# Attention and Mish feed-forward on one core: loads one pair further ahead, and the first pair's q and k turned earlier

## The chip, the cores and the metric

The kernel runs on one NeuronCore of a Trainium2 chip. The metric is the device time of one execution in microseconds. A core has TensorE (PE), VectorE (DVE), ScalarE (ACT), GpSimd (POOL) and SyncE (SP); SP computes nothing here and issues most of the DMA transfers.

## The reference

```python
# q, k, v: (8, 12, 448, 64) float32; w_in: (768, 2048); w_out: (2048, 768)
scores = scale * np.matmul(q, k.transpose(0, 1, 3, 2))
m = np.max(scores, axis=-1, keepdims=True)
e = np.exp(scores - m)
attn = e / (np.sum(e, axis=-1, keepdims=True) + np.exp(-m) + 1e-09)
attn_out = np.matmul(attn, v)
x = attn_out.transpose(0, 2, 1, 3).reshape(3584, 768)
h = x @ w_in
g = h * np.tanh(softplus(h))      # Mish
out = g @ w_out                   # (3584, 768) float32
```

## The kernel before

The 96 heads are worked in 48 pairs, three pairs to a unit, so that a batch item is two units: units 0 to 15 hold attention, units 16 to 19 only what remains of the feed-forward. Units are counted from 0, so the eighth unit is unit 7. A unit u starts with pair p0 = 3u, and nxt = p0 + 3 is the first pair of the next unit.

**A pair's way in.** `load_pair` (line 158) issues three loads on SP's queue, one each for q, k and v, into buffers of which there are four of each kind. `cast_pair` (lines 201 to 207, with `cast_v`, 188) casts them to bf16 on GpSimd into `qk_bf`, which has room for six pairs. Then q and k must be turned so that the head's 64 channels lie on the partitions. That is done in one of two ways:

- `transpose_pair` (line 224) does eight transposes on TensorE into two PSUM banks, and `evac_qk` copies them out: q on VectorE, scaled (line 263), k on ScalarE (line 271).
- `turn_by_dma` (line 237) does it with one DMA transpose on SP's queue, straight from `qk_bf` to `qk_all`. `TURN_BY_DMA` lists the pairs for which it is used: every unit's first pair from pair 21 on, and pair 46.

`rest_of` (lines 245, 246) then makes on GpSimd two small copies that the fourth score step needs.

**The joined units.** Units 6 to 15 follow an order written out by hand, the list `JOINED`. Its entries are emitted one after the other: "s" the score matmuls of a step (lines 304, 307, 312), "m" the row maxima (line 335), "e" the exponentials (line 347), "fill" two matmuls' worth of the output product w_out (line 543), "copy" its evacuation (line 522) and, where rows are complete, the stores (line 507), "av" and "avc" the product with v of the unit before (line 423) and its evacuation (line 432), "load" a `load_pair` and, for arguments 1 and 2, a `cast_pair` one pair behind, "turn" a `turn_by_dma` if the pair is in the list. Every engine, and SP's queue, works off its own part in the order of emission.

**The Mish stage.** Behind the list come eight steps f = 0 to 7 of the product with w_in and Mish (lines 442, 469, 481). Into them are woven: at f = 0 the denominators (line 363) and the normalisation of the first pair on VectorE (line 386), and the DMA transpose of the normalised pair into `eT` (line 390) on SP; at f = 1, 3 and 5 the transposes and evacuations of the next unit's first, second and third pair, as far as they are not turned by DMA, and at f = 1 a `cast_pair`; at f = 3 the second pair's normalisation and the `rest_of` of a pair turned by DMA; at f = 4 the third pair's normalisation, which GpSimd does (line 384). Each normalisation is followed by its transpose into `eT`. At f = 7 the first three score steps of the next unit are emitted.

In a unit of even number, the first two steps of Mish are emitted together at f = 0 (`mm1_mish_first`), and f = 1 has no matmul of its own. In the joined units the PSUM bank of step f is given by a list, and the transposes go to banks 4 (q) and 2 (k) at f = 1 and 5, and to 5 and 3 at f = 3:

```python
    JOINED_MISH_BANK = (7, 0, 4, 2, 6, 1, 7, 6)
```

`LEAD` is 4. In the joined units before, "load" with argument a loads pair p0 + a + 3 and casts pair p0 + a + 2 (for a of 1 and 2); the cast at f = 1 is that of pair p0 + 5. So a unit loads and casts exactly the three pairs of the unit that follows.

Of the kernel before, what the change touches and what calls it, by code (L numbers as in the profile page):

```python
# [15 lines left out]
UNIT_PAIRS = 3  # L16
# [3 lines left out]
def kernel(  # L20
# [27 lines left out]
    N_PAIRS = B * HP  # L48
# [63 lines left out]
    for t_ in en_bufs:  # L112
# [4 lines left out]
    GROUP_FROM = 2 * HP  # L117
    JOINED_FROM = 2 * UNITS_PER_B + 2
    ONE_COPY = range(1, HP + UNIT_PAIRS)
    TURN_BY_DMA = tuple(  # L120
        p
        for p in range(GROUP_FROM + 3 * UNIT_PAIRS, N_PAIRS)
        if p % UNIT_PAIRS == 0 or p == N_PAIRS - UNIT_PAIRS + 1
    )
    SCALED_IN_CAST = (*ONE_COPY, *TURN_BY_DMA)
# [23 lines left out]
    def load_pair(p, which="qkv"):  # L149
        if p >= N_PAIRS:  # L150
            return
        b, h0 = p // HP, (p % HP) * 2
        tiles = loaded.setdefault(p, [])
        for nm, src in (("q", q), ("k", k), ("v", v)):
            if nm not in which:
                continue
            t = ld_pool.tile([SP_, 2, NT * D], FP32, tag=f"{nm}_f", name=f"{nm}_f")
            nc.sync.dma_start(
                out=t, in_=src[b, h0 : h0 + 2].rearrange("h (p t) d -> p h (t d)", t=NT)
            )  # L160
            tiles.append(t)
# [25 lines left out]
    def cast_v(p):  # L187
        nc.gpsimd.tensor_copy(out=casted[p][2], in_=loaded.pop(p)[2])  # L188

    def cast_pair(p, with_v=True):  # L190
        if p >= N_PAIRS:
            return
        q_f, k_f = loaded[p][:2]
        q_bf, k_bf = (qk_bf[:, p % N_CAST, i] for i in range(2))
        v_bf = bf_pool.tile([SP_, 2, NT * D], BF16, tag="v_bf", name="v_bf")
        by_t = "p h (t d) -> p t h d"
        cast_q, cast_k = nc.gpsimd.tensor_copy, nc.gpsimd.tensor_copy
        if p == 0:
            cast_q, cast_k = nc.vector.tensor_copy, nc.scalar.copy
        if p not in SCALED_IN_CAST:  # L200
            cast_q(out=q_bf, in_=q_f.rearrange(by_t, t=NT))  # L201
        else:
            nc.gpsimd.tensor_scalar(  # L203
                out=q_bf, in0=q_f.rearrange(by_t, t=NT),
                scalar1=SCALE, scalar2=1.0, op0=ALU.mult, op1=ALU.mult,
            )
        cast_k(out=k_bf, in_=k_f.rearrange(by_t, t=NT))  # L207
        casted[p] = (q_bf, k_bf, v_bf)
        if with_v:
            cast_v(p)  # L210
# [23 lines left out]
    def turn_by_dma(p):  # L234

        qk = qk_all[:, p % UNIT_PAIRS]
        nc.sync.dma_start_transpose(
            out=qk.rearrange("c s (t q) -> c (s t) q", q=SP_),
            in_=qk_bf[:, p % N_CAST].rearrange("q s t h d -> q (s t h d)"),
        )  # L240
        qkT[p] = qk[:, 0, :], qk[:, 1, :]
# [40 lines left out]
    def scores(idx):  # L282
        score_maxima(*score_products(idx))
# [45 lines left out]
    def score_maxima(st, s, at, heads=(0, 1)):  # L329
        sc, cols = st["sc", s]  # L330
        maxima = [(st["negm"][:, c : c + 1], sc[bk][:, 0:S]) for bk, c in enumerate(cols) if bk in heads]
        if len(cols) == 2 and sc_pairs[at] is not None:
            maxima = [(st["negm"][:, s : s + 5 : 4], sc_pairs[at][:, :, 0:S])]
        for negm, scored in maxima:
            nc.vector.tensor_reduce(out=negm, in_=scored, axis=AX.X, op=ALU.max, negate=True)  # L335
# [22 lines left out]
    def expm_of(p):  # L358
        w = att[p]["whole"]
        nc.scalar.activation(out=w["expm"], in_=w["negm"], func=AF.Exp)  # L360
# [205 lines left out]
    first_mm2 = 2 * UNITS_PER_B  # L566
# [5 lines left out]
    for g in range(B // 2):  # L572
# [51 lines left out]
    )  # L624
    JOINED = (
        ("mA", 1), ("fill", 2), ("mA", 0), ("fill", 1), ("mB", 0), ("fill", 1), ("eA", 1),
        ("load", 0), ("mB", 1), ("fill", 2), ("eA", 0), ("mB", 2), ("fill", 1), ("eB", 1),
        ("mA", 2), ("fill", 2), ("eB", 0), ("fill", 1), ("copy", 0), ("fill", 3), ("eB", 2),
# [4 lines left out]
        ("fill", 1), ("mB", 6), ("fill", 1), ("eA", 4), ("fill", 1), ("copy", 1), ("s", 11),  # L633
        ("eB", 6), ("load", 2), ("fill", 1), ("m", 11), ("fill", 1), ("eB", 5), ("fill", 1),
# [4 lines left out]
    )  # L639
# [12 lines left out]
    LEAD = UNIT_PAIRS + 1  # L652
# [68 lines left out]
    for u in range(UNITS_PER_B, N_UNITS + 2 * UNITS_PER_B):  # L721
# [10 lines left out]
        nxt = p0 + UNIT_PAIRS  # L732
# [5 lines left out]
        for what, arg in JOINED if joined else ():  # L738
            at, idx = p0 + arg, p0 * STEPS + arg
            heads = {"A": (0,), "B": (1,)}.get(what[-1], (0, 1))  # L740
            if what == "s":
                held[arg] = score_products(idx)
            elif what[0] == "m":
                score_maxima(*held[arg], heads)
            elif what[0] == "e":
                exps(idx, heads)
            elif what == "fill":
                for _ in range(arg):
                    filler.popleft()[0]()
            elif what == "copy":  # L750
                for evac in copies[arg]:
                    evac()
            elif what == "av":
                held["av", arg] = av_pair(at - UNIT_PAIRS, bank=joined_banks[AV_BANK[arg]])
            elif what == "avc":
                held["av", arg]()
            elif what == "load":
                load_pair(at + LEAD - 1)
                if arg:
                    cast_pair(at + LEAD - 2)  # L760
            elif nxt + arg in TURN_BY_DMA:
                turn_by_dma(nxt + arg)
        if joined:
            expm_of(nxt - 1)

        for n in () if joined else range(steps):
            pi, s = divmod(n, STEPS)
            p, idx = p0 + pi, p0 * STEPS + n
# [4 lines left out]
            if grouped:  # L773
# [14 lines left out]
                if n in LOAD_AT:  # L788
                    at = p0 + LOAD_AT.index(n)
# [51 lines left out]
        for f in range(FF_U):  # L841
            first_scores = f == FF_U - 1 and to_group and nxt < N_PAIRS
            if first_scores and u + 1 < JOINED_FROM:
                for s in range(3):
                    scores(nxt * STEPS + s)
            if moe:
                first = to_group and nxt == GROUP_FROM
                bank, ff = sc_banks[0][0] if f == 1 else None, w * FF_U + f
                if joined:
                    bank = joined_banks[JOINED_MISH_BANK[f]]  # L850
                elif to_group:
                    at = (FIRST_MISH_BANK if first else MISH_BANK)[f]
                    if at is not None:
                        bank = (sc_banks[0][1], None, mo_tiles[1], sc_banks[0][0])[at]
                if not joined or w or f >= MISH_AHEAD:
                    mm1_mish(b, FIRST_ORDER[f] if first else ff, bank)
                elif f == 0:
                    mm1_mish_first(b, [joined_banks[at] for at in JOINED_MISH_BANK[:MISH_AHEAD]])
                if f == 2 and to_gather:
                    gather_mid(to_gather.popleft())  # L860
            if first_scores and u + 1 >= JOINED_FROM:
                held = {s: score_products(nxt * STEPS + s) for s in range(3)}
            if u == UNITS_PER_B and f == 2:
                load_w(5)
            if not attn:
                continue
            if f == 0:
                denominators(att[p0]["whole"])
                normalise(todo[0], dma=todo[0] not in BY_PE)
            if f in (1, 3, 5):  # L870
                if nxt + f // 2 not in TURN_BY_DMA:
                    transpose_pair(nxt + f // 2, bank=f // 2 % 2)
                    evac_qk(nxt + f // 2)
                if f == 1 and u >= first_mm2:
                    cast_pair(nxt + UNIT_PAIRS - 1)
            if not to_group and f in (4, 6):
                scores_ahead(nxt * STEPS + f // 2 - 1)
            if f == FF_U - 1 and not to_group:
                scores_ahead(nxt * STEPS + 3)
            if f == 3:  # L880
                normalise(todo[1], dma=todo[1] not in BY_PE)
                for p in TURN_BY_DMA:
                    if p // UNIT_PAIRS == u + 1:
                        rest_of(p)
            if f == 4:
                normalise(todo[2], dma=todo[2] not in BY_PE, on_pool=u + 1 < N_UNITS)
# [39 lines left out]
```

## Time and profile before

| | us |
|---|---|
| median of three runs | 461.14 (459.6 to 462.93) |
| the profiled execution | 464.11 |
| its span, first to last instruction | 462.3 |
| TensorE busy | 427.4 |
| ScalarE busy | 342.1 |
| VectorE busy | 340.9 |
| GpSimd busy | 187.3 |
| mean granted TensorE clock | 0.987 of full speed |

In the rows of the profile "PE b L442 x6" means six matmuls from line 442 that write a tile named b; the number ahead is the start in us from the span's start, the next the time that the group took. In brackets stands the idle time of the engine before it, and what ended that. In the table by stretches each row has the stretch, its length, then busy time and count of PE, PEld, DVE, ACT and POOL, the granted clock, the DMA engines' busy share and GB/s. The ends of matmuls are modelled and overlap the next one's start, so start-to-start distances say more than durations.

### The profile page before, as it was taken

How to read it: one execution, taken by the hardware profiler on the slowest of the kernel's cores; microseconds unless marked ns; L12 is line 12 of the kernel's file. 1: busy time of each engine (PE TensorE's matmuls, PEld its weight loads, DVE VectorE, ACT ScalarE, POOL GpSimd, SP SyncE). 2: the span in 40 equal slices, each digit the busy share in tenths (PEclk: the TensorE clock that was granted, in tenths of full speed). 3: DMA queues.
4: the chain of work that ended last, by engine and by line, in shares of the span. 5: the costliest groups of instructions: out<-in, count | busy, mean ns of one | idle time of the engine just before them, and what ended most of it. 6: DMA issues, size and time to landing. Idle time of an engine off the chain costs nothing.

```text
span 462.3 us, 8732 instructions
## 1 busy us (share of the span) xinstructions
PE 427.4 (92%) x2968; PEld 234.3 (51%) x2968; DVE 340.9 (74%) x756; ACT 342.1 (74%) x908; POOL 187.3 (41%) x352
## 2 busy tenths in 40 slices
PE   4596798869999999899999999999999999999996
PEld 2243445434545655455555555455555455555565
DVE  4899978948887888868788888788888888421121
ACT  5998978967797979778888788798988888311300
POOL 4666655652616253353627171625454360000000
PEclk9997999999999999999999999999999999999999
DMA  8999999999999999999999999999999995950213
GB/s 229 207 200 221 255 151 215 221 199 216 195 246 238 207 210 204 264 194 278 199 244 231 219 234 209 271 206 238 227 270 205 255 203 137 171 137 0 69 35 102
DMA packets 211661, 92.66 MB, mean 200 GB/s; under 512 B 168352, under 2 KB 208160, under 8 KB 211616
## 3 DMA queue, kind: packets, MB, share of 16 engines
q1 hardware_dynamic: 204032, 85.76, 87.9%
q0 software_dynamic: 7488, 6.29, 9.4%
q8 instruction: 23, 0.38, 0.4%
q14 instruction: 22, 0.18, 0.1%
q10 hardware_dynamic: 96, 0.05, 0.0%
HBM read 45.61 MB, written 11.01 MB: 122 GB/s over the span
## 4 chain that ended last, share of the span: by engine, by line
PE 65%; DMA 16%; DVE 5%; ACT 5%; issue 3%; SPq 3%; POOL 2%; POOLq 0%; DVEq 0%; ACTq 0%
PE mo L543 25%; PE mo L442 15%; DMA q_f<-in_q_dram 7%; PE b L442 6%; PE b L543 5%; PE b L304 4%; ACT en L347 4%; DMA k_f<-in_k_dram 4%; DMA eT<-en 4%; DVE negm L335 3%; PE b L423 2%; PE mo L423 2%; PE b L224 2%; DMA qk_all<-qk_bf 1%; SPq L390 1%
## 5 line engine op out<-in xcount | busy, mean ns | idle before, releaser
L347 ACT ACTIVATE en<-b,negm 128x448 bf16<-128x448 f32 x216 | 133.9, 636 | 25.7 <-DVE negm L335 25.7
L335 DVE TENSOR_REDUCE negm<-b 128x1 f32<-128x448 f32 x216 | 120.9, 616 | 20.0 <-PE b L307 20.0
L543 PE MATMUL mo<-w_out_sb,gT 128*128 128x384 bf16 (+3 forms) x736 | 108.7, 300 | 1.4 <-DVE o_sb L522 0.7
L543 PEld LDWEIGHTS <-gT 128*128 128x128 bf16 x896 | 82.6, 98 | 51.8 <-issue 10.8
L442 PEld LDWEIGHTS <-w_in_sb 128*128 128x128 bf16 x768 | 72.3, 98 | 66.5 <-issue 5.5
L442 PE MATMUL mo<-xT,w_in_sb 128*128 128x448 bf16 x480 | 101.1, 353 | 0.8 <-DVE xT L432 0.3
L481 ACT ACTIVATE gT<-mo 128x448 bf16<-128x448 f32 x73 | 40.3, 552 | 52.1 <-PE mo L442 52.0
L384 POOL TENSOR_SCALAR en<-en,rden 128x448 bf16<-128x448 bf16 x109 | 67.3, 634 | 19.5 <-DVE rden L378 11.8
L386 DVE TENSOR_SCALAR en<-en,rden 128x448 bf16<-128x448 bf16 x227 | 71.8, 386 | 0.7
L442 PE MATMUL b<-xT,w_in_sb 128*128 128x448 bf16 x282 | 58.7, 352 | 0.0
L347 ACT ACTIVATE en<-sc,negm 128x448 bf16<-128x448 f32 x84 | 52.5, 642 | 3.9 <-DVE negm L335 2.6
L522 DVE COPY o_sb<-mo 128x384 f32<-128x384 f32 (+3 forms) x54 | 25.8, 494 | 40.1 <-PE mo L543 39.4
L335 DVE TENSOR_REDUCE negm<-sc 128x2 f32<-128x896 f32 (+1 forms) x48 | 45.4, 969 | 6.4 <-PE sc L307 4.0
L203 POOL TENSOR_SCALAR qk_bf<-q_f 112x512 bf16<-112x512 f32 x18 | 11.1, 615 | 88.1 <-DMA q_f<-in_q_dram 88.1
L347 ACT ACTIVATION_READ_ACCUMULATOR en<-b,negm 128x1 f32 x216 | 45.0, 208 | 0.0
L201 POOL CAST qk_bf<-q_f 112x512 bf16<-112x512 f32 x29 | 19.7, 679 | 44.6 <-DMA q_f<-in_q_dram 44.2
L188 POOL CAST v_bf<-v_f 112x512 bf16<-112x512 f32 x48 | 30.1, 626 | 15.0 <-DMA v_f<-in_v_dram 14.7
L207 POOL CAST qk_bf<-k_f 112x512 bf16<-112x512 f32 x47 | 29.3, 623 | 7.6 <-DMA k_f<-in_k_dram 6.4
L423 PEld LDWEIGHTS <-v_bf 112*64 112x64 bf16 x384 | 20.1, 110 | 23.4 <-issue 9.0
L224 PEld LDWEIGHTS <-qk_bf 112*128 112x128 bf16 x304 | 19.6, 104 | 21.7 <-POOL qk_bf L207 4.6
L304 PE MATMUL b<-qk_all 64*128 64x448 bf16 x108 | 29.3, 358 | 0.3 <-DMA qk_all<-qk_bf 0.3
L307 PE MATMUL b<-qk_all 64*128 64x448 bf16 x108 | 29.3, 358 | 0.0
(71 smaller groups left out, 524.7 us busy)
## 6 DMA issues: line engine op xcount, KB each, us to landing
q_f<-in_q_dram SPq DMA_DIRECT2D x48, 224.0 KB, 5.4
k_f<-in_k_dram SPq DMA_DIRECT2D x48, 224.0 KB, 5.6
v_f<-in_v_dram SPq DMA_DIRECT2D x48, 224.0 KB, 5.6
w_in_sb<-in_moe_w_in_dram POOLq DMA_DIRECT2D x12, 256.0 KB, 6.3
w_out_sb<-in_moe_w_out_dram POOLq DMA_DIRECT2D x8, 384.0 KB, 6.9
out_dram<-o_sb SPq DMA_DIRECT2D x7, 336.0 KB, 5.2
out_dram<-o_sb SPq DMA_DIRECT2D x8, 288.0 KB, 4.9
out_dram<-o_sb SPq DMA_DIRECT2D x8, 240.0 KB, 5.2
```

What stands on the lines that cost most here:

```text
L188: nc.gpsimd.tensor_copy(out=casted[p][2], in_=loaded.pop(p)[2])
L207: cast_k(out=k_bf, in_=k_f.rearrange(by_t, t=NT))
L304: nc.tensor.matmul(sc[0][:, 0:S], lhsT=qT[0:64, qa : qa + 128], rhs=kA, start=True, stop=True)
L307: nc.tensor.matmul(sc[1][:, 0:S], lhsT=qT[64:128, qb : qb + 128], rhs=kB, start=True, stop=True)
L335: nc.vector.tensor_reduce(out=negm, in_=scored, axis=AX.X, op=ALU.max, negate=True)
L347: nc.scalar.activation(out=st["en"][:, :, c, 0:SP_], in_=sc[bk][:, 0:S].rearrange("q (j c) -> q j c", j=NT), func=AF.Exp, bias=st["negm"][ ...
L384: nc.gpsimd.tensor_scalar(scalar2=1.0, op0=ALU.mult, op1=ALU.mult, **args)
L386: nc.vector.tensor_scalar(scalar2=None, op0=ALU.mult, **args)
L423: nc.tensor.matmul(av[h * 64 : (h + 1) * 64, 0:S], lhsT=v_bf[:, h, j * D : (j + 1) * D], rhs=e_h, start=(j == 0), stop=(j == NT - 1),)
L442: nc.tensor.matmul(h_ps[:, 0:S], lhsT=w_in_sb[:, dm, ff * 128 : (ff + 1) * 128], rhs=xT[b][:, dm, :], start=(dm == 0), stop=(dm == DM_T - 1),)
L481: nc.scalar.activation(out=gT[b][:, ff, :], in_=h_ps[:, 0:S], func=AF.Mish)
L543: nc.tensor.matmul(st["o"][:, st["at"] : st["at"] + nq * NQ], lhsT=src[:, ff, c0 : c0 + 128], rhs=w_out_sb[:, ff, q0 * NQ : (q0 + nq) * NQ ...
```

## The change

Four things are edited, and they hang together.

1. Pair 21, the first pair of unit 7, leaves the list of pairs turned by DMA; unit 6 transposes it on TensorE at f = 1.
2. In `JOINED`, ("turn", 0) moves from near the end to just behind ("s", 3), and ("load", 0) moves from near the start to right behind it. On SP's queue the turn then follows the three transposes into eT, and the loads follow the turn.
3. From unit 7 on a "load" loads one pair further ahead, p0 + a + 4, and casts p0 + a + 3; the cast at f = 1 is that of pair p0 + 6. So the first pair of a unit is loaded and cast one unit earlier than the others.
4. Unit 6 makes up for the step: at ("turn", 1) it loads pair 24, and at f = 1 it casts pairs 23 and 24.

```diff
-        for p in range(GROUP_FROM + 3 * UNIT_PAIRS, N_PAIRS)
+        for p in range(GROUP_FROM + 4 * UNIT_PAIRS, N_PAIRS)
...
         ("mA", 1), ("fill", 2), ("mA", 0), ("fill", 1), ("mB", 0), ("fill", 1), ("eA", 1),
-        ("load", 0), ("mB", 1), ("fill", 2), ("eA", 0), ("mB", 2), ("fill", 1), ("eB", 1),
+        ("mB", 1), ("fill", 2), ("eA", 0), ("mB", 2), ("fill", 1), ("eB", 1),
         ("mA", 2), ("fill", 2), ("eB", 0), ("fill", 1), ("copy", 0), ("fill", 3), ("eB", 2),
-        ("fill", 3), ("s", 3), ("eA", 2), ("fill", 1), ("m", 3), ("s", 5), ("s", 4), ("s", 6),
+        ("fill", 3), ("s", 3), ("turn", 0), ("load", 0), ("eA", 2), ("fill", 1), ("m", 3), ("s", 5),
+        ("s", 4), ("s", 6),
...
-        ("eA", 10), ("av", 0), ("avc", 1), ("eA", 8), ("turn", 0), ("av", 2), ("avc", 0),
+        ("eA", 10), ("av", 0), ("avc", 1), ("eA", 8), ("av", 2), ("avc", 0),
...
             elif what == "load":
-                load_pair(at + LEAD - 1)
+                lead = LEAD - 1 if u == JOINED_FROM else LEAD
+                load_pair(at + lead)
                 if arg:
-                    cast_pair(at + LEAD - 2)
+                    cast_pair(at + lead - 1)
             elif nxt + arg in TURN_BY_DMA:
                 turn_by_dma(nxt + arg)
+            elif u == JOINED_FROM and arg == 1:
+                load_pair(nxt + UNIT_PAIRS)
...
-                if f == 1 and u >= first_mm2:
+                if f == 1 and first_mm2 <= u <= JOINED_FROM:
                     cast_pair(nxt + UNIT_PAIRS - 1)
+                if f == 1 and u >= JOINED_FROM:
+                    cast_pair(nxt + UNIT_PAIRS)
```

## The prediction

> **What bounds the kernel now.** I read the busy table first, then the stretches of the joined stage one unit at a time, then the waits of TensorE.
>
> ```profile
> PE 427.4 (92%) x2968; PEld 234.3 (51%) x2968; DVE 340.9 (74%) x756; ACT 342.1 (74%) x908; POOL 187.3 (41%) x352
> ```
>
> TensorE is the engine to watch. The share alone doesn't say where it waits, so I cut the span at the first score matmul (line 304) of each unit. Each row below is one unit, units 6 to 14; after the length stands TensorE's busy time.
>
> ```profile
> 149.00:173.41 24.41, 24.41 (x175) 13.55 (x175) 21.11 (x48) 20.91 (x56) 9.93 (x21) 1.00 1.00 208
> 173.41:199.84 26.43, 24.74 (x175) 13.47 (x175) 20.53 (x47) 21.01 (x56) 12.22 (x24) 1.00 1.08 235
> 199.84:224.63 24.79, 24.47 (x174) 13.54 (x174) 20.72 (x48) 21.19 (x57) 10.05 (x19) 1.00 1.08 214
> 224.63:249.81 25.18, 24.74 (x173) 13.38 (x174) 21.07 (x47) 20.73 (x56) 12.06 (x25) 1.00 1.13 245
> 249.81:274.36 24.55, 24.55 (x174) 13.56 (x174) 20.96 (x48) 21.02 (x56) 11.74 (x23) 1.00 1.03 228
> 274.36:299.52 25.16, 24.57 (x174) 13.55 (x174) 21.01 (x47) 21.02 (x56) 11.65 (x24) 1.00 1.16 236
> 299.52:324.32 24.80, 24.58 (x175) 13.49 (x175) 21.16 (x48) 21.01 (x56) 9.95 (x20) 1.00 1.08 219
> 324.32:348.71 24.39, 24.39 (x174) 13.59 (x173) 20.55 (x47) 20.91 (x56) 12.31 (x26) 1.00 1.11 251
> 348.71:373.48 24.77, 24.35 (x166) 13.08 (x166) 21.18 (x47) 20.57 (x55) 11.44 (x22) 1.00 1.11 233
> ```
>
> Units 6 and 13 last 24.41 and 24.39 us and TensorE is busy through all of them: 24.39 us is the floor of a unit with two pairs transposed on TensorE. The others are longer by 2.04, 0.40, 0.79, 0.16, 0.77, 0.41 and, in unit 14, 0.38. That is the whole pool from which earlier loads can pay. What it consists of is seen where the long unit 7 stops, and at the start of unit 9:
>
> ```profile
> 193.91 1.30 PE L442 MATMUL b<-xT,w_in_sb 128*128 128x448 bf16 x6
> 196.71 0.37 PE L224 MATMUL b<-ident,qk_bf 112*128 112x112 bf16 x4 [1.50 <-POOL qk_bf L201]
> ...
> 190.87 0.61 POOL L201 CAST qk_bf<-q_f 112x512 bf16<-112x512 f32 x1
> 195.58 1.07 POOL L201 CAST qk_bf<-q_f 112x512 bf16<-112x512 f32 x1 [2.79 <-DMA q_f<-in_q_dram]
> ...
> 224.63 0.36 PE L304 MATMUL b<-qk_all 64*128 64x448 bf16 x1 [0.32 <-DMA qk_all<-qk_bf]
> ```
>
> The transposes of a unit's third pair wait for GpSimd's cast, the cast for its load; once the scores wait for the turned pair. The chain of waits agrees: in this stage it runs through loads, casts and the turn wherever it leaves TensorE.
>
> **What the change takes away.** From unit 7 on, the third pair to be transposed gets its cast at the place of the second one before: in unit 7 that is 190.87 instead of 195.58, against a need at 195.04 (six matmuls from 193.91, 0.19 us each, which is 1.13). Even 1.3 us later it would be in time. The turn is issued some 8 us earlier. So all seven excesses should go: 2.04 + 0.40 + 0.79 + 0.16 + 0.77 + 0.41 + 0.38 = 4.95. Unit 14 has one pair fewer on TensorE and its own floor lies lower by the step of eight transposes, 0.39 (the first two rows of the next fence): together **5.3 us gained**. The lower end is 3 us, if only the waits that TensorE's rows name go.
>
> **What it adds in unit 6.** Pair 21 leaves the list of pairs turned by DMA. Its eight transposes now stand in the Mish stage of unit 6 behind f = 1, write banks 4 and 2 of the joined banks, and are evacuated by VectorE (q, line 263) and ScalarE (k, line 271). The next matmuls in program order, f = 2, write bank 4 again, and f = 3 bank 2 (JOINED_MISH_BANK). In no unit of the trace from 6 on did transposes stand there, so the cost is worked out from the order of the engines:
>
> ```profile
> 167.98 0.56 PE L224 MATMUL b<-ident,qk_bf 112*128 112x112 bf16 x8
> 168.37 1.30 PE L442 MATMUL mo<-xT,w_in_sb 128*128 128x448 bf16 x6
> ...
> 165.14 3.00 PE L442 MATMUL b<-xT,w_in_sb 128*128 128x448 bf16 x15
> ...
> 165.51 0.63 ACT L347 ACTIVATE en<-b,negm 128x448 bf16<-128x448 f32 x1
> 166.73 0.23 ACT L360 ACTIVATE expm<-negm 128x21 f32<-128x21 f32 x1
> ...
> 166.99 0.18 DVE L363 SCALAR_TENSOR_TENSOR den<-sums,expm 128x21 f32<-128x21 f32 x1 [1.15 <-ACT expm L360]
> 167.53 2.90 DVE L386 TENSOR_SCALAR en<-en,rden 128x448 bf16<-128x448 bf16 x7
> ...
> 167.97 0.62 POOL L201 CAST qk_bf<-q_f 112x512 bf16<-112x512 f32 x1 [1.00 <-DMA q_f<-in_q_dram]
> ...
> 268.43 1.89 DVE L386 TENSOR_SCALAR en<-en,rden 128x448 bf16<-128x448 bf16 x7
> 270.58 0.38 DVE L263 TENSOR_SCALAR qk_all<-b 128x448 bf16<-128x448 bf16 x1
> ```
>
> Of the fifteen matmuls from 165.14 the first three belong to f = 0; f = 2 starts at 165.14 + 3 x 0.19 = 165.71. There the new transposes go in: q at once, k after the second-last exp (ends near 166.1) has read bank 2. VectorE reaches the evacuation only after the denominators (166.99, behind expm) and the seven normalisations of the first pair (line 386), which are emitted at f = 0. Those take 2.90 us here beside GpSimd's casts, 1.89 us in unit 10, where GpSimd was idle for most of them. After the change GpSimd has rest_of(21), which needs that same evacuation, queued ahead of the cast at 167.97, so it sits idle: I take 1.89. Evacuation 169.4 to 169.75, f = 2 at about 169.8: **4.1 us lost**, 0.39 of it work. Upper end 5.1 with 2.90; no lower end, since VectorE works in order. Behind it the extra cast of pair 24 on GpSimd and its three loads (in the place of the turn of pair 21 on SP) lie beside TensorE's later f's; k's evacuation at 169.2 on ScalarE precedes f = 3. No idle time follows in unit 6 that could absorb it.
>
> **The clock.** A gap that long costs more than itself in one place of this trace:
>
> ```profile
> 97.90:101.60 3.70, 0.04 (x1) 0.00 (x0) 1.06 (x3) 3.32 (x12) 1.47 (x3) 1.00 1.24 221
> 102.50:105.90 3.40, 3.40 (x14) 1.15 (x13) 1.40 (x3) 0.11 (x1) 0.00 (x0) 0.50 1.11 206
> ...
> 194.69:198.10 3.41, 1.72 (x15) 0.85 (x14) 2.38 (x8) 1.51 (x4) 2.46 (x5) 1.00 1.23 214
> ```
>
> After 3.7 us without matmuls the granted clock was 0.50 for 3.4 us (1.7 us of work lost); after unit 7's gap of 1.67 us it stayed 1.00. Ours is 4.1 us with eight transposes at its head. Ends 0 and 1.7; I take **1.0 lost**, since part of the slow stretch can fall inside the gap. The Trainium skill, page "TensorE: Matmul & The Clock Gate", section "Part 1: The HAM clock gate", says that the array falls to half rate after an idle window of about 3.4 us, and that the window runs free of the kernel; the 3.7 us row agrees. By that rule the fall hangs on where the window lies in each execution, so that the sum below would be 0.7 us higher with a full fall and 1.0 lower with none.
>
> **What it moves.** In SP's queue the turn now stands between the last eT transpose and the loads; load 0 stands behind it. SP and DMA are close to full there:
>
> ```profile
> 279.04 4.90 SPq L390 DMA_TRANSPOSE eT<-en  x1
> 284.00 0.57 SPq L158 DMA_DIRECT2D q_f<-in_q_dram  x1
> ...
> 259.43 0.58 SPq L158 DMA_DIRECT2D q_f<-in_q_dram  x1
> 267.37 1.34 SPq L237 DMA_TRANSPOSE qk_all<-qk_bf  x1
> ...
> 270.08 1.05 POOL L201 CAST qk_bf<-q_f 112x512 bf16<-112x512 f32 x1 [1.36 <-DMA q_f<-in_q_dram]
> ...
> 295.19 0.61 POOL L201 CAST qk_bf<-q_f 112x512 bf16<-112x512 f32 x1 [2.26 <-DMA q_f<-in_q_dram]
> 298.67 4.31 POOL L384 TENSOR_SCALAR en<-en,rden 128x448 bf16<-128x448 bf16 x7
> ...
> 286.87 1.68 PE L423 MATMUL mo<-eT,v_bf 112*64 112x448 bf16 x16
> ...
> eT<-en SPq DMA_TRANSPOSE x43, 6.8
> ```
>
> This is a ring: last eT transpose ends (283.94), nine loads, the third one cast (295.19: 11.2 us; in unit 10, 259.43 to 270.08, 10.7), then GpSimd normalises (3.5 later), 4.3, and the next last eT transpose can be issued, 4.9. That is 23.4 to 23.9 us. The turn now stands in it with 1.3: 24.7 to 25.2 us, against TensorE's 24.39. So the last eT comes later by 0.3 to 0.85 us in each unit, six times from unit 8 on: 1.8 to 5.1 us. The slack that it eats first: issued 279.04, landed 6.8 later at 285.8, wanted by the last eight of the sixteen matmuls from 286.87, at 287.6: 1.8 us. Left: 0 to 3.3; I take **1.0 lost**, nearer the lower end, since GpSimd also stops waiting for the turn itself. No wait of SP is new: the turn's target in qk_all is free after ("s", 3), some 5 us into a unit, while SP gets there 9 us in; its cast is one unit old. The f = 1 cast holds up the same things on GpSimd as before.
>
> **Sum.** +4.1 + 1.0 + 1.0 - 5.3 = **+0.8 us**. On the profiled execution, 464.11 us with a span of 462.3, that is 464.9; the median of the three runs is 461.14, 3 us lower, so I forecast **461.9 us**. One per cent, 4.6 us, is about what can be told from no change.
>
> **Rivals.**
> 1. *The ring becomes the bound.* If a turn between the transposes and the loads holds the DMA up by more than its 1.3 us of issue, say 2.3, the ring takes 25.7 to 26.2 and the period with it. It decides from 24.39 us on, once the 1.8 us are eaten: 6 x (1.3 to 1.8) - 1.8 = 6 to 9 lost in place of 1.0, +5.8 to +8.8 in all: 467 to 470. For it: DMA shares of 1.03 to 1.16 in every unit. Against it: the eT is nowhere waited for in units 7 to 14. Chance 0.15.
> 2. *The stall in unit 6 is not there or is covered*, for instance if VectorE gets to the evacuation sooner than I read. Then -5.3 + 1.0, at best -5.3: 455.8 to 456.8. Against it: VectorE's order. Chance 0.08.
> 3. *The change doesn't do what it says*: the casts stay late, as each waits in GpSimd's queue for loads that start 1.3 us later behind the turn, and only 1 to 2 us of the 5.3 go. Then +4 to +5: 465 to 466. Against it: the second cast's margin in unit 7, whose q is done at 191.48, with k's behind it, 3 us ahead of the need. Chance 0.07.
>
> The forecast with its own terms (clock 0 to 1.7, ring 0 to 3.3, stall to 5.1) has 0.70, and 459.9 to 465.9. To hold 8 in 10 I let the range run from 458.8 to 466.0. Faster by over 1% (under 456.5) 0.05, slower by over 1% (over 465.75) 0.17, within 0.78.
>
> **What would show it.** In unit 6 of the changed trace: a gap of TensorE of 3 to 4 us before f = 2, its releaser VectorE's line 263, and a clock row of 0.5 behind it or none. Units 7 to 14 at 24.4 us, no waits of line 224 for qk_bf. The last eT of a unit creeping towards the matmuls of line 423; waits of line 423 for eT would show the ring. The forecast is wrong if unit 6 shows no gap, or if units 8 to 14 stay above 24.8.

## The result and the profile after

The changed kernel takes 466.6 us (median of 20 runs), the kernel before 463.12 us in the runs beside it. The ratio is 1.0076 with a 95% interval of 1.0054 to 1.0099: 0.8% slower, some 3.5 us.

The whole loss can be read from the stage that was edited. This is the table by stretches of the changed kernel, units 6 to 14, cut as before at each unit's first score matmul:

```profile
147.67:177.74 30.07, 26.80 (x182) 14.52 (x182) 20.42 (x49) 21.78 (x57) 13.95 (x28) 0.94 0.99 210
177.74:202.14 24.40, 24.40 (x174) 13.54 (x174) 20.74 (x47) 20.91 (x56) 9.35 (x20) 1.00 0.88 203
202.14:226.54 24.40, 24.40 (x174) 13.58 (x174) 21.26 (x45) 21.02 (x56) 9.26 (x18) 1.00 1.16 230
226.54:251.90 25.36, 24.66 (x175) 13.62 (x175) 22.46 (x50) 21.04 (x56) 11.55 (x23) 1.00 1.11 232
251.90:276.87 24.97, 24.77 (x175) 13.61 (x175) 21.99 (x49) 20.93 (x56) 10.54 (x22) 1.00 1.04 220
276.87:301.73 24.86, 24.57 (x175) 13.57 (x175) 21.17 (x50) 20.91 (x56) 10.95 (x22) 1.00 1.11 235
301.73:326.48 24.75, 24.75 (x174) 13.63 (x175) 21.58 (x44) 21.03 (x56) 11.88 (x23) 1.00 1.07 235
326.48:351.96 25.48, 24.57 (x174) 13.53 (x173) 22.57 (x52) 21.02 (x56) 11.32 (x24) 1.00 1.10 230
351.96:376.04 24.08, 24.08 (x166) 13.31 (x167) 21.24 (x49) 20.54 (x55) 11.18 (x24) 1.00 1.07 211
```

Unit 6 went from 24.41 to 30.07 us: 5.66 lost. Units 7 to 14 went from 200.07 us together (173.41 to 373.48) to 198.30 (177.74 to 376.04): 1.77 won. That is +3.89 us. A unit with two pairs on TensorE takes 24.39 us where nothing is waited for, and unit 14 takes 24.00; by that the floor of units 7 to 14 is 194.73 us, and they stand 3.57 us over it. Outside the stage the two executions differ by -1.33 ahead of unit 6 and +0.24 behind unit 14, which leaves the 2.8 us between the spans, 462.3 and 465.1.

What TensorE waits for from 140 us on, in the waits of the changed kernel (line of the waiting work, releaser, us in total, times, longest; idle times under 0.15 us are left out):

```profile
PE b L442 <- DVE qk_all L263: 3.1, 1, 3.1
PE b L304 <- DVE qk_all L263: 1.9, 3, 0.9
PE b L423 <- DMA eT<-en: 0.9, 1, 0.9
```

The waits of transposes for casts are gone from the list. Both new waits are for VectorE's evacuation of q, line 263. The third one lies behind unit 14 and was there before. The list counts too little, because the modelled end of one matmul hides the start of a wait. Start to start, against units 7 and 8, the scores slip by 0.87, 0.28, 0.45 and 1.07 us in units 9, 10, 11 and 13, 2.67 us in all; the products with v slip by 0.5 us behind eT, and one transpose by 0.19 us behind its cast (unit 12). These are nearly all of the 3.57 us.

The first new wait stands in unit 6. TensorE, then VectorE, in order of time, then the stretch behind the gap:

```profile
164.38 0.36 PE L224 MATMUL b<-ident,qk_bf 112*128 112x112 bf16 x4
164.95 0.36 PE L224 MATMUL b<-ident,qk_bf 112*128 112x112 bf16 x4 [0.21 <-ACT en L347]
168.36 4.11 PE L442 MATMUL b<-xT,w_in_sb 128*128 128x448 bf16 x12 [3.05 <-DVE qk_all L263]
172.31 0.56 PE L224 MATMUL b<-ident,qk_bf 112*128 112x112 bf16 x8
...
166.20 1.81 DVE L386 TENSOR_SCALAR en<-en,rden 128x448 bf16<-128x448 bf16 x7
167.93 0.38 DVE L263 TENSOR_SCALAR qk_all<-b 128x448 bf16<-128x448 bf16 x1
...
168.30:171.80 3.50, 3.44 (x11) 1.44 (x11) 0.34 (x2) 0.58 (x2) 3.30 (x7) 0.55 1.06 157
```

The transposes begin at 164.38, where f = 2 would have begun, and f = 2 begins at 168.36: 3.98 us. Its twelve matmuls (f = 2 and 3) then reach to 172.31, which is 3.95 us instead of 2.27, at a granted clock of 0.55: another 1.68 us. Together they are the 5.66.

The second new wait is met first in the scores that are emitted at the end of unit 8 (in the table, the start of unit 9). TensorE, VectorE and GpSimd of the changed kernel, and at the end the normalisation's step over units 7 to 14, before and changed (behind the first bar the busy time in us and the mean of one in ns):

```profile
226.54 0.36 PE L304 MATMUL b<-qk_all 64*128 64x448 bf16 x1
227.80 0.35 PE L304 MATMUL b<-qk_all 64*128 64x448 bf16 x1 [0.70 <-DVE qk_all L263]
...
221.09 2.87 DVE L386 TENSOR_SCALAR en<-en,rden 128x448 bf16<-128x448 bf16 x7
224.51 2.86 DVE L386 TENSOR_SCALAR en<-en,rden 128x448 bf16<-128x448 bf16 x7
227.37 0.38 DVE L263 TENSOR_SCALAR qk_all<-b 128x448 bf16<-128x448 bf16 x1
...
221.48 0.66 POOL L201 CAST qk_bf<-q_f 112x512 bf16<-112x512 f32 x1 [0.78 <-DMA q_f<-in_q_dram]
224.92 0.64 POOL L203 TENSOR_SCALAR qk_bf<-q_f 112x512 bf16<-112x512 f32 x1 [1.33 <-DMA q_f<-in_q_dram]
...
L386 DVE TENSOR_SCALAR en<-en,rden 128x448 bf16<-128x448 bf16 x112 | 36.7, 396 | 0.3
L386 DVE TENSOR_SCALAR en<-en,rden 128x448 bf16<-128x448 bf16 x112 | 41.7, 441 | 0.3
```

GpSimd casts one pair beside VectorE's first normalisation and one beside the second. Both normalisations take 2.9 us; the one in unit 6, with GpSimd idle, took 1.81. The q of the third pair is evacuated behind them, at 227.75, and the third score step, due at 226.93, starts at 227.80. The kernel before had some of this already (396 ns a step; its two normalisations here took 2.52 and 1.88 us), but there VectorE was done with q at 223.7, ahead of the scores' need.

### The profile page after: what moved, and what is told of

The parts are those of the page before. It is cut to its first block, busy times and chain, and to the rows that moved or that the text cites. A ratio compares the mean times of both kernels' runs of the same rounds, so it can differ in the third digit from the quotient of the medians.

```text
span 465.1 us, 8744 instructions
## 1 busy us (share of the span) xinstructions
PE 433.7 (93%) x2976; PEld 238.9 (51%) x2976; DVE 346.5 (74%) x757; ACT 342.7 (74%) x909; POOL 186.1 (40%) x352
## 4 chain that ended last, share of the span: by engine, by line
PE 69%; DVE 13%; ACT 8%; DMA 5%; issue 2%; POOL 1%; SPq 1%; POOLq 0%; ACTq 0%; DVEq 0%
PE mo L543 24%; PE mo L442 15%; PE b L442 10%; ACT en L347 7%; DVE negm L335 5%; PE b L543 5%; PE b L304 4%; DVE en L386 4%; PE mo L423 4%; DMA eT<-en 3%; DMA k_f<-in_k_dram 3%; PE b L423 2%; PE b L224 2%; PE mo L312 1%; DVE xT L432 1%
## 5 line engine op out<-in xcount | busy, mean ns | idle before, releaser
L347 ACT ACTIVATE en<-b,negm 128x448 bf16<-128x448 f32 x216 | 133.9, 636 | 21.6 <-DVE negm L335 21.5
L543 PE MATMUL mo<-w_out_sb,gT 128*128 128x384 bf16 (+3 forms) x736 | 107.5, 298 | 1.5 <-DVE o_sb L522 0.9
L386 DVE TENSOR_SCALAR en<-en,rden 128x448 bf16<-128x448 bf16 x227 | 75.7, 402 | 0.7
L442 PE MATMUL b<-xT,w_in_sb 128*128 128x448 bf16 x282 | 60.6, 360 | 3.1 <-DVE qk_all L263 3.1
L423 PEld LDWEIGHTS <-v_bf 112*64 112x64 bf16 x384 | 20.9, 113 | 21.0 <-issue 11.1
L224 PEld LDWEIGHTS <-qk_bf 112*128 112x128 bf16 x312 | 20.8, 106 | 17.1 <-DVE qk_bf L201 4.1
L423 PE MATMUL mo<-eT,v_bf 112*64 112x448 bf16 x232 | 28.7, 381 | 0.6 <-DVE eT L405 0.6
```

Source lines behind the costliest of these rows:

```text
L224: nc.tensor.transpose(by_s[s][:, t * SP_ : (t + 1) * SP_], src[:, t].rearrange("p h d -> p (h d)"), ident[:SP_, :SP_],)
L347: nc.scalar.activation(out=st["en"][:, :, c, 0:SP_], in_=sc[bk][:, 0:S].rearrange("q (j c) -> q j c", j=NT), func=AF.Exp, bias=st["negm"][ ...
L386: nc.vector.tensor_scalar(scalar2=None, op0=ALU.mult, **args)
L423: nc.tensor.matmul(av[h * 64 : (h + 1) * 64, 0:S], lhsT=v_bf[:, h, j * D : (j + 1) * D], rhs=e_h, start=(j == 0), stop=(j == NT - 1),)
L442: nc.tensor.matmul(h_ps[:, 0:S], lhsT=w_in_sb[:, dm, ff * 128 : (ff + 1) * 128], rhs=xT[b][:, dm, :], start=(dm == 0), stop=(dm == DM_T - 1),)
L543: nc.tensor.matmul(st["o"][:, st["at"] : st["at"] + nq * NQ], lhsT=src[:, ff, c0 : c0 + 128], rhs=w_out_sb[:, ff, q0 * NQ : (q0 + nq) * NQ ...
```

## The experiments

My theory after these readings had two parts. In unit 6 the banks of pair 21's transposes are wanted again too early, and the clock falls behind the gap. In units 7 to 14 the turn ahead of the loads delays the casts, which then run beside the normalisations. The rivals were that unit 6 loses by its extra loads and casts, and that units 7 to 14 wait for the ring of eT transposes, turn and loads. Ratios are to the kernel before on the same chip, with the 95% interval in brackets; they are not the quotients of the medians.

**One part alone: pair 21 on TensorE, nothing else.**

```diff
 # the kernel before
-        for p in range(GROUP_FROM + 3 * UNIT_PAIRS, N_PAIRS)
+        for p in range(GROUP_FROM + 4 * UNIT_PAIRS, N_PAIRS)
```

> The kernel before with one part of the change alone: pair 21 is transposed on TensorE in unit 6, nothing is loaded or turned earlier. Theory (the transposes' banks 4 and 2 are wanted again at once, and VectorE comes to the evacuation only after seven normalisations): unit 6 as in the changed kernel, about 30 us instead of 24.4, with a gap of 3 us or more before f = 2 released by line 263, and a granted clock of 0.5 behind it; units 7 to 14 keep their waits of before, 200 us in all. Sum +5 to +6 us, 1.1 to 1.3% slower than before. Since here the cast of pair 23 isn't followed by that of pair 24, the gap should be the same. Rival (the loss in unit 6 comes from the extra loads and the extra cast of pair 24): unit 6 stays near 24.8 us and the time within 0.5 us of before.

Measured: 467.19 us, ratio 1.0062 (1.0026 to 1.0098). Unit 6 and, further down, the end of unit 11 in its stretches and timeline:

```profile
148.09:178.17 30.08, 26.80 (x182) 14.53 (x182) 20.45 (x49) 21.80 (x57) 12.18 (x25) 0.94 0.91 185
...
301.21 0.37 PE L224 MATMUL b<-ident,qk_bf 112*128 112x112 bf16 x4 [1.72 <-POOL qk_bf L201]
301.76 0.37 PE L224 MATMUL b<-ident,qk_bf 112*128 112x112 bf16 x4 [0.19 <-POOL qk_bf L207]
301.97 4.12 PE L442 MATMUL mo<-xT,w_in_sb 128*128 128x448 bf16 x12
...
302.00:305.50 3.50, 3.50 (x14) 1.47 (x12) 0.11 (x1) 1.08 (x2) 3.25 (x9) 0.54 1.06 212
```

Unit 6 takes 30.08 us, as in the changed kernel (30.07), without any extra load or cast: the rival falls. The median's loss of 3.45 us is less than the 5 to 6 expected; that the clock doesn't fall behind the gap in every execution (below) may be why. The rows of unit 11 show a late cast costing twice: the wait, and then the half clock; with it units 7 to 14 took 201.96 us, where I had expected 200.

**That part undone: pair 21 by DMA again, the rest as changed.** The kernel was run in two batches.

```diff
 # the changed kernel
-        for p in range(GROUP_FROM + 4 * UNIT_PAIRS, N_PAIRS)
+        for p in range(GROUP_FROM + 3 * UNIT_PAIRS, N_PAIRS)
...
-        ("eA", 10), ("av", 0), ("avc", 1), ("eA", 8), ("av", 2), ("avc", 0),
+        ("eA", 10), ("av", 0), ("avc", 1), ("eA", 8), ("turn_first", 0), ("av", 2), ("avc", 0),
...
+            elif what == "turn_first":
+                if u == JOINED_FROM:
+                    turn_by_dma(nxt)
+            elif what == "turn" and u == JOINED_FROM and arg == 0:
+                pass
```

> The changed kernel with that one part undone: pair 21 is turned by DMA in unit 6, at the turn's old place, while pair 24 is loaded ahead and all later units are as changed. Theory: unit 6 at 24.4 us, clock 1.00 through it, units 7 to 14 as in the changed kernel at 198 to 199 us together against 200 before: -1 to -2 us against before, ratio 0.996 to 0.999. Rival (the early turn and loads lose as much in units 7 to 14 as they gain, and the changed kernel's gain there was only slack left by the stall of unit 6): 200 us or more in units 7 to 14, ratio 1.000 to 1.005.

> The changed kernel with pair 21 turned by DMA once more. In its first profile units 7 to 14 took 203.3 us, with 3.7 us of waits for eT and a fall of the clock in unit 7. Theory (without the stall of unit 6 SP's ring of transposes, turn and loads has no head start, so that the last transpose into eT is late from unit 7 on): waits for eT of 1 us or more in all again, units 7 to 14 at 199 to 203 us. Rival (that profile was an outlier): 198 to 198.5 us as in the kernel with bank 1, waits for eT of 0.5 us.

Measured: 462.49 us, ratio 0.9979 (0.9944 to 1.0015), then 462.14 us, 0.9964 (0.9922 to 1.0005). Unit 6, units 7 to 14 together, and a wait in the latter, of the second run:

```profile
147.68:172.09 24.41, 24.41 (x175) 13.54 (x175) 21.27 (x47) 20.95 (x56) 10.77 (x19) 1.00 1.08 236
172.09:371.74 199.65, 196.15 (x1378) 108.42 (x1378) 169.94 (x381) 167.38 (x447) 90.73 (x178) 1.00 1.09 228
...
PE mo L423 <- DMA eT<-en: 3.2, 4, 1.4
```

Unit 6 is whole again at 24.41 us, at full clock. But units 7 to 14 keep almost nothing, 199.65 us against 200.07: now the last eT is late, 3.2 us in four waits. (Two executions differ here; the first one's numbers stand in the expectation above.) So the ring is real, and in units 7 to 14 the rival came nearer than my theory of 198 to 199 us; by the ratios neither run can be told from the kernel before. The rival's reason, that the stall of unit 6 hides the ring by giving SP a head start, is not shown. SP issues the last eT transpose 1.9 us into unit 7 in the changed kernel and 5.7 us into it here, but in unit 8 it is 6.8 and 6.5 us, and the next kernel has no stall either and waits for eT only 0.5 us. Why the waits are longer here stays open.

**The transposes of pair 21 in another bank.** Bank 1 is wanted again only at f = 5.

```diff
 # the changed kernel
-                    transpose_pair(nxt + f // 2, bank=f // 2 % 2)
+                    if u == JOINED_FROM and f == 1:
+                        transpose_pair(nxt, alone=joined_banks[1])   # q and k in its two halves
+                    else:
+                        transpose_pair(nxt + f // 2, bank=f // 2 % 2)
```

> The changed kernel with the eight transposes of pair 21 put into bank 1, which is wanted again only at f = 5, instead of banks 4 and 2. Theory: no gap before f = 2, unit 6 at 24.8 to 25.2 us (0.39 us of transposes and a short wait for the exponential that reads bank 1), clock 1.00; with units 7 to 14 at 198 to 199 us the sum is -1 us against before, ratio 0.996 to 1.000. Rival (TensorE would wait there for something else, for instance the casts or ScalarE): unit 6 stays at 28 us or more and the ratio above 1.005.

Measured: 462.89 us, ratio 0.9934 (0.9896 to 0.9972); the medians, 462.89 against 463.74, differ by 0.2% only, so the stretches say more here. Its unit 6, units 7 to 14 together, and the waits in these (lines stand 3 higher in this kernel and the next two: 266 is the evacuation of q, 389 the normalisation, 307 the scores, 426 the product with v):

```profile
144.37:169.64 25.27, 25.02 (x182) 13.94 (x181) 22.12 (x49) 21.48 (x57) 11.30 (x22) 1.00 1.07 236
169.64:367.87 198.23, 195.87 (x1377) 108.08 (x1378) 173.47 (x381) 167.15 (x447) 89.07 (x175) 1.00 1.07 228
...
PE b L307 <- DVE qk_all L266: 1.6, 3, 0.9
PE mo L426 <- DMA eT<-en: 0.5, 1, 0.5
```

Unit 6 at 25.27 us instead of 30.07, clock 1.00: with the same transposes, loads and casts, the bank alone decides 4.8 us. Of these 1.7 are the half clock, which didn't follow the gap in every execution (last run below); against an execution without it, 28.39 us, the bank decides 3.1. Units 7 to 14 stay where they were in the changed kernel, 198.23 against 198.30.

**The cast behind the normalisation.** In the kernel with bank 1, the cast of the pair loaded ahead goes behind GpSimd's own normalisation.

```diff
 # the kernel with bank 1
-                if f == 1 and u >= JOINED_FROM:
-                    cast_pair(nxt + UNIT_PAIRS)
...
                 normalise(todo[2], dma=todo[2] not in BY_PE, on_pool=u + 1 < N_UNITS)
+                if u >= JOINED_FROM:
+                    cast_pair(nxt + UNIT_PAIRS)
```

> The kernel of the run before with the cast of the pair loaded one unit ahead moved on GpSimd from f = 1 to behind the third pair's normalisation, so that it meets neither of VectorE's two normalisations. Theory (GpSimd's casts, which the later loads push beside VectorE's normalisations, slow these from 1.8 to 2.9 us each, and the third score step then waits for the q that line 263 evacuates behind them): the second normalisation takes 1.8 to 2.2 us again, the waits of line 304 for line 263 vanish, and units 7 to 14 come to 195 to 196.5 us: 2 to 3 us less than the run before, ratio 0.990 to 0.994. Rival (the ring of transposes, turn, loads and cast sets the waits): the last transpose into eT comes earlier here too, but the waits of line 304 for line 263 stay, as does the second normalisation's 2.8 us.

> The kernel with pair 21 in bank 1 and the late cast once more, beside the changed kernel on one chip. Theory: 5.5 us saved in unit 6 and 1.3 us in units 7 to 14 against the changed kernel, so 1.3 to 1.6% under it, and 0.6 to 0.9% under the kernel before. Rival (the first comparison's 0.9886 was the luck of few runs): not below before by more than 0.4%.

Measured: 460.23 us, ratio 0.9886 (0.9835 to 0.9937), and 460.82 us, 0.9954 (0.9920 to 0.9989) in the second batch, beside the changed kernel's 469.02: 1.7% under that. Under the kernel before it was 0.5%, less than the 0.6 to 0.9 that I had expected. So the first ratio was partly luck, as the rival had it, though the gain is clear. Units 7 to 14 of the first run, the normalisation there, and the waits left:

```profile
173.66:370.70 197.04, 195.92 (x1377) 108.39 (x1376) 169.14 (x379) 167.23 (x447) 88.12 (x173) 1.00 1.09 231
...
L389 DVE TENSOR_SCALAR en<-en,rden 128x448 bf16<-128x448 bf16 x112 | 39.1, 417 | 0.3
...
PE mo L426 <- DMA eT<-en: 0.8, 2, 0.5
```

The waits of the scores are gone and a normalisation's step has a mean of 417 ns (459 in the kernel with bank 1). I had expected 195 to 196.5 us; 0.8 us of waits for eT remain: the ring again.

**The turn at its old place.** In the kernel with bank 1, and in the one with the late cast.

```diff
 # the kernel with bank 1; the same edit in the one with the late cast
-        ("mB", 1), ("fill", 2), ("eA", 0), ("mB", 2), ("fill", 1), ("eB", 1),
+        ("load", 0), ("mB", 1), ("fill", 2), ("eA", 0), ("mB", 2), ("fill", 1), ("eB", 1),
...
-        ("fill", 3), ("s", 3), ("turn", 0), ("load", 0), ("eA", 2), ("fill", 1), ("m", 3), ("s", 5),
+        ("fill", 3), ("s", 3), ("eA", 2), ("fill", 1), ("m", 3), ("s", 5),
...
-        ("eA", 10), ("av", 0), ("avc", 1), ("eA", 8), ("av", 2), ("avc", 0),
+        ("eA", 10), ("av", 0), ("avc", 1), ("eA", 8), ("turn", 0), ("av", 2), ("avc", 0),
```

> The kernel with bank 1 (pair 21's transposes moved away from banks 4 and 2, loads one pair ahead), with the turn and load 0 put back to their old places in the list, so that the loads go out about 1.3 us earlier and the turn behind them. Theory (the later loads are what brings the casts beside VectorE's normalisations): casts 1 to 2 us earlier in the unit, the second normalisation at 2.0 to 2.7 us instead of 2.9 to 3.1, the waits of line 304's step (released by q's evacuation) at under 0.8 us in all, against 1.6 us in the kernel with bank 1, units 7 to 14 at 196.5 to 197.8 us. Against that stands a wait of GpSimd for the turn's landing, which may give part of it back. Rival (the place of the turn doesn't matter, the casts collide because one more pair is loaded ahead): units 7 to 14 within 0.5 us of 198.2 and the same waits.

> The kernel with the cast behind the third normalisation, with the turn and load 0 put back to their old places too. Theory: what the late cast frees is already free, so the turn's place can give only the earlier casts of the other two pairs beside the first normalisation: units 7 to 14 at 195 to 197 us, against 197.0 with the early turn, and a ratio to before within 0.003 of that kernel's. Rival (the early turn pays, since GpSimd doesn't have to wait for it before the third normalisation): 0.5 us or more above 197.0, with waits of GpSimd's line 245 for the turn.

Measured: 459.38 us, ratio 0.9948 (0.9910 to 0.9986), and 459.07 us, 0.9935 (0.9898 to 0.9973). Units 7 to 14 of the first, and all its waits of TensorE there:

```profile
176.40:372.24 195.84, 195.33 (x1377) 107.98 (x1376) 170.10 (x381) 167.07 (x447) 89.66 (x175) 1.00 1.09 233
...
PE b L307 <- DMA qk_all<-qk_bf: 0.3, 1, 0.3
```

195.84 us is 1.1 over the floor of 194.73 (seven units of 24.39 and unit 14's 24.00), 2.4 under the kernel with bank 1, and better than I expected: no wait for VectorE or eT is left in the list. The casts come earlier, as the theory had it: in unit 9 the casts of the three pairs begin 14.2, 17.9 and 21.5 us into the unit, against 17.1, 20.9 and 23.8 in the changed kernel. The step of a normalisation still has a mean of 420 ns, so it isn't its length alone that counts, but when VectorE is through with it. So the loads one pair ahead pay, and the turn moved ahead of them is what took most of it back. With both edits units 7 to 14 took 196.61 us, with 1.3 us of waits for the turn itself; the times of the two kernels can't be told apart. Both beat the kernel before and the changed one.

**GpSimd beside VectorE, by itself.** Three copies of no use to the output, 112x512 on GpSimd, added to the kernel with the turn at its old place: once at f = 0, beside the normalisations, once behind the third normalisation.

```diff
 # the kernel with bank 1 and the turn at its old place; first run:
                 normalise(todo[0], dma=todo[0] not in BY_PE)
+                if u > JOINED_FROM:
+                    for _ in range(3):
+                        nc.gpsimd.tensor_copy(out=spare_out, in_=w_in_sb[:SP_, 0, 0:512])
 # second run: the same three lines behind normalise(todo[2], ...) instead
```

> The kernel with bank 1 and the turn at its old place, plus three copies on GpSimd (112x512, of no use to the output) in every unit from 7 to 15, emitted at f = 0, so that they and the cast behind them run beside VectorE's two normalisations. Theory (GpSimd's work beside VectorE's normalisation slows it, and the third score step pays): the mean of a normalisation's step on VectorE rises from 433 to 450 ns or more, waits of the score line for the q evacuation come back with 0.5 to 2 us in all, units 7 to 14 at 196.5 to 198.5 us against 195.8. Rival (the waits came from the turn's place through the transposes into eT, not from GpSimd's casts): no waits of scores for the evacuation, units 7 to 14 within 0.4 us of 195.8 or longer only by waits for eT.

> The control: the same three copies emitted behind the third normalisation, where GpSimd is idle for the next ten us and VectorE takes maxima out of PSUM. Theory: nothing changes, normalisation steps at 425 to 440 ns, units 7 to 14 within 0.4 us of 195.8, no waits of scores for the evacuation. Rival (any more work on GpSimd costs time): 1 us or more above 195.8.

Measured: 467.92 us, ratio 1.0052 (1.0007 to 1.0097), and 458.11 us, 0.9884 (0.9816 to 0.9953; four runs only). Units 7 to 14, normalisation and waits with the copies beside (lines 4 higher than before: 267, 308, 390):

```profile
174.83:377.36 202.53, 196.06 (x1377) 108.19 (x1377) 178.28 (x378) 168.14 (x447) 102.91 (x196) 1.00 1.07 222
...
L390 DVE TENSOR_SCALAR en<-en,rden 128x448 bf16<-128x448 bf16 x111 | 48.0, 500 | 0.3
...
PE b L308 <- DVE qk_all L267: 3.9, 4, 1.5
PE b L308 <- DMA qk_all<-qk_bf: 1.8, 2, 1.3
PE mo L427 <- DMA eT<-en: 0.8, 1, 0.8
```

and with the copies behind:

```profile
171.54:366.82 195.28, 195.00 (x1378) 108.10 (x1378) 167.22 (x381) 167.18 (x447) 102.97 (x196) 1.00 1.10 233
...
L390 DVE TENSOR_SCALAR en<-en,rden 128x448 bf16<-128x448 bf16 x112 | 36.5, 396 | 0.3
```

GpSimd does the same work in both (102.9 and 103.0 us). Beside the normalisations a step of VectorE takes 500 ns and TensorE waits 3.9 us at the scores; behind them the step takes 396 ns and there is no such wait (the kernel without copies has 420 ns). This is the mechanism that the rows of unit 8 suggested. The whole price, 7.25 us between the two, came out larger than I had expected, and not all of it is this mechanism: 2.6 us are waits for the turn and for eT. The copies also stand ahead of other work in GpSimd's queue, and I haven't separated the two.

**The changed kernel again.**

> The changed kernel again, to have it on the same chip as the three others and to see whether the half clock behind the gap in unit 6 comes back. Theory: unit 6 at 28.4 us without a fall of the clock, or up to 30.1 us with it, ratio 1.005 to 1.010. Rival (the fall of the clock in two of two profiles was chance): no fall here.

Measured: 469.02 us, ratio 1.0105 (1.0043 to 1.0167). Unit 6, the stretch behind its gap, and two waits in units 7 to 14:

```profile
145.27:173.66 28.39, 25.12 (x182) 14.03 (x181) 21.05 (x49) 21.80 (x57) 13.14 (x26) 1.00 1.01 222
166.00:170.00 4.00, 4.00 (x28) 2.25 (x28) 1.54 (x4) 1.56 (x4) 3.88 (x8) 1.00 1.04 172
...
PE mo L423 <- DMA eT<-en: 1.4, 3, 0.9
PE b L304 <- DVE qk_all L263: 0.9, 2, 0.5
```

Here the clock held at 1.00 behind the same gap of 3.1 us, and unit 6 took 28.39 us, 1.68 less than with the fall. So the rival held: the fall doesn't come in every execution. In units 7 to 14 the ring and VectorE share the waits, and their sum comes out the same: 198.14 us.

## Why the prediction was right and wrong

The forecast was 461.9 us, a loss of 0.8. The loss was 3.5, and 466.6 lies 0.6 over the range. A sign that it named for being wrong showed as well: of units 8 to 14 four took over 24.8 us (9, 10, 11 and 13). Some 2 us of the distance in absolute time are not the change's: the median of three runs to which I added the sum was 461.14, and twenty runs of the same kernel have 463.12.

- *The pool of 5.3 us in units 7 to 14*: right in size. The waits for casts vanished but for a slip of 0.2 us, and in the kernel with the turn put back the stage came to within 1.1 us of the floor.
- *Unit 6, 4.1 us lost at bank 4*: right in place, chain and size, 3.98. VectorE's normalisation took 1.81 us with GpSimd idle, for the reason given. The run with bank 1 shows that it is the bank.
- *The clock, 1.0 taken between 0 and 1.7*: right in kind. Both ends occurred, 1.68 in one profile and 0 in another of the same kernel. The reason given for 1.0, that part of the slow stretch falls inside the gap, isn't borne out: where the clock fell, it was after the gap, and the whole 1.68 us was paid.
- *The ring, 1.0 taken between 0 and 3.3*: right as a mechanism, seen with 1.4 us of waits in one profile of the changed kernel and 3.2 where pair 21 was turned by DMA again. In the profile of the result it cost 0.5 us, in slips too short for the list of waits.
- *What was wrong*: the sentence "The f = 1 cast holds up the same things on GpSimd as before", in the part on what the change moves. I asked who waits behind GpSimd and not who runs beside it. The same later loads that feed the ring move the casts later: in unit 9 they begin 17.1, 20.9 and 23.8 us into the unit, where the kernel before has 13.3, 17.4 and 21.3, and VectorE's two normalisations run from 19.1 to 25.2. So all three casts run into the normalisations, not the last two alone. I had used exactly this contention to price unit 6, 1.89 against 2.90 us, and left it out for the eight units behind it. The third score step paid 2.67 us for it in four units, a term that the sum puts at nothing. With the ring's 0.5 and some small slips, units 7 to 14 stood 3.57 us over their floor where I allowed 1.0: -5.34 + 3.57 is the -1.77 measured. With unit 6, 3.98 + 1.68, that makes the +3.89 of the stage.
- *The rivals*: the ring as the bound, at 467 to 470, had the direction, but not the mechanism in this profile: a unit stood 0.45 us over its floor on average (3.57 over eight), not 1.3 or more, and most of that was VectorE's. The stall of unit 6 was there, so the second fell. The third, with 0.07 the least likely, came nearest: the casts are late behind the turn, 1.77 us of the 5.3 went, and +3.89 is close to its +4 to +5. Only the way differs, over VectorE to the scores and not over the transposes.

## What to carry to other kernels

When transfers move, follow not only who waits for them but what their consumers then run beside; an engine that is idle for half of the span can still cost time by when it works. Before a transpose or any other short product is put between two larger ones, look where its PSUM bank is wanted next and what the evacuating engine has queued ahead: here one bank index was worth 3.1 us, and 4.8 where the half clock followed. And judge an edit by the stretch of the trace that it touches: units 7 to 14 of the changed kernel took 198.30 and 198.14 us in its two profiles, while whole runs of the kernel before spread from 459.59 to 466.92 us.

## What the hardware showed that I had not expected

The granted clock falls after much shorter gaps than the 3.7 us in the trace of before. In the run with pair 21 alone, waits of 1.72 and 0.19 us around four transposes were followed by a stretch of 3.5 us at 0.54, and twelve matmuls took 4.05 us start to start instead of 2.37. In the trace of before, a gap of 1.50 us in the same place was followed by none; and behind unit 6's gap of 3.1 us the clock fell in one profile of the changed kernel and held in another. Whether it falls isn't fixed by the kernel, and each of these two falls cost some 1.7 us. Ahead of unit 6 the kernels here run the same work, and yet unit 6 begins at 144.37 us in the kernel with bank 1 and at 151.12 us in the one with the turn put back; the clock from 100 us on was 1.00 in the first and 0.93 in the second. The traces show what came first: in the run with the turn put back TensorE waited 3.3 us for eT in unit 4 and the half clock followed, so that this unit took 29.4 us; in the kernel with bank 1 it has no such wait there and takes 23.5. So waits for eT with a fall behind them are one source of the spread between these runs. Why they come in one execution and not in another stays open.
